# Placing the loaded rows of a convolution on other partitions, in more and partly longer transfers

## The chip, the cores and the metric

The kernel runs on one core of one Trainium2 chip. The metric is device time in microseconds (us) of one execution. Each kernel was run several times; the profile of one of those executions is read below. An execution that took over 1.5% longer than the fastest of its kernel is called slow, the others fast; comparisons are between fast ones. The granted clock is the share of full speed that TensorE's clock was granted, as the profile shows it.

Engines are named as in the profile: PE is TensorE's matmuls and PEld its weight loads, DVE is VectorE, ACT ScalarE, POOL GpSimd, SP SyncE. SPq, ACTq and so on are the sequencers that issue DMA transfers. A line number such as L174 is a line of the kernel profiled, so the same code has another number in another kernel.

## The reference, cut to what matters

```python
# x (8, 5696, 128), h (5696, 128), float32
Xf = np.fft.rfft(x, n=2 * S, axis=1)
Hf = np.fft.rfft(h, n=2 * S, axis=0)
y = np.fft.irfft(Xf * Hf[None], n=2 * S, axis=1)[:, :S, :]     # long convolution
x2 = y.reshape(8 * 5696, 128)
logits = x2 @ phi                                               # 32 slots
d = softmax over the 45568 rows;  slot_input = d.T @ x2
slot_out = relu(slot_input @ w1[e]) @ w2[e]                     # per expert
c = softmax over the slots;       out = c @ slot_out            # (45568, 128)
```

## The kernel before

The convolution is done as matrix products over 5,696 = 89 x 64 rows. One *step* handles one chunk of one sequence: it loads x (89 rows to 89 partitions, two runs of 2 KB each), folds it on GpSimd, multiplies it on TensorE and stores the result f to memory. A second stage loads f again as g, multiplies with the transform of h and stores z. A third stage loads z (90 rows) for two chunks at a time and goes on from there; two steps are a *pair*. There are 72 steps (h, then eight sequences of eight chunks) and 32 pairs of the third stage. Nearly all transfers are issued by SP.

```python
SPLIT = R1 // 16 * 16                    # 80 of R1 = 89 rows
Z0, X0, F0, F1 = 20, 20, 6, 82           # first partitions
...
xcs = [apool.tile([P, 2, CH, D], F32, name=f"xc{i}", ...) for i in range(3)]
def load_x(c):
    ...
    for r in (slice(0, SPLIT), slice(SPLIT, R1)):        # 80 rows, then 9
        v = src[r, CH * j:CH * (j + 1), :]
        v = bass.AP(tensor=v.tensor, offset=v.offset,
                    ap=[v.ap[0], [gap * D, 2], [1, CH * D]])
        nc.sync.dma_start(
            out=t_[X0 + r.start:X0 + r.stop, :, :, :].rearrange("p s n d -> p s (n d)"), in_=v)
...
def stage_b2(u):
    ...
    st = bpool.tile([P, 2, 2 * D], F32, name="zst", tag="zst", bufs=3)
    nc.scalar.activation(st[:, 0:n, :], bz[:, 0:n, 0:2 * D], AF.Copy)
    nc.sync.dma_start(out=zd[g - 1]..., in_=st[:, 0:n, :])          # the z store
...
def load_z(c):                                            # one chunk, 90 rows, runs of 8 KB
    ...
    nc.sync.dma_start(out=t_[Z0:Z0 + N1, :, :, :, :]..., in_=zd[b]...[:, j * w_:(j + 1) * w_])

def load_pair(T):
    if T < NT:
        load_z(2 * T)
        load_z(2 * T + 1)
...
for t in range(steps):
    ...
    if pair(1 - 2 * ahead) is not None:
        load_pair(pair(1 - 2 * ahead))                    # z, in every second step
    if t < NA:
        load_x(t + 3)                                     # x of three steps later
        stage_a(t, 0)                                     # its f stores come next
        fold(t + 1, 0)
    ...
```

The order of the calls is the order on SP's queue: first z, then x, then the f stores, then loads of g and stores of z. In the trace of before, its 977 transfers, 973 of SP and 4 of ScalarE, name eight completion semaphores strictly in turn, and 914 of SP's 973 wait, in the instruction or just ahead of it, for the semaphore that they then name, which is that of the transfer eight before. I read this as at most **eight in flight**.

Of the kernel before, what the change touches and what calls it, by code (L numbers as in the profile page):

```python
# [10 lines left out]
F32 = mybir.dt.float32  # L11
# [3 lines left out]
PSUM = bass.MemoryType.PSUM  # L15


def transform_tables(S, N1, N2, CH, Z0, X0, F0, F1):












    N, R1, HALF, P = N1 * N2, S // N2, N2 // 2, 2 * N2
    k1 = np.arange(N1)
    alpha = np.pi * (k1 + 0.5) / N1
    m1 = np.arange(R1) - (N1 - 1) / 2
    a1 = np.outer(m1, alpha)
    s1 = np.stack([np.cos(a1), -np.sin(a1), -np.cos(a1)], 1)
    a0 = np.outer(alpha, np.arange(N1 // 2) + 0.5)
    i1 = np.stack([np.cos(a0), -np.sin(a0), -np.cos(a0)], 1)
    NP = N1 // 2
    part = s1  # L40
    s1 = np.zeros((P, 3, P))
    for a, p in enumerate((F0, F1)):
        s1[X0:X0 + R1, :, p:p + NP] = part[:, :, a * NP:(a + 1) * NP]
    i1 = np.pad(i1[np.arange(N1).reshape(2, N1 // 2).T.reshape(-1)],
                [(Z0, P - N1 - Z0), (0, 0), (0, N2 - N1 // 2)])
    k2 = np.arange(N2)
    omega = np.pi * (k1[:, None] + 2 * N1 * k2[None] + 0.5) / N
    m2 = np.arange(HALF) - (N2 - 1) / 2
    a2 = m2[None, :, None] * omega[:, None, :]
    w = np.concatenate([np.cos(a2), np.sin(a2)], 1)  # L50
    back = np.arange(N2).reshape(2, HALF // CH, CH).transpose(1, 0, 2).reshape(-1)
    NU = (NP + 1) // 2
    turn = (N1 - 1) / 2 * alpha[:, None] + (N2 - 1) / 2 * omega
    wq = np.zeros((2, N2, NP, N2))
    vq = np.zeros((2, N2, NU, 2, N2))
    tn = np.zeros((2, N2, 2, NU, 2))
    for a in range(2):
        wq[a] = w[a * NP:(a + 1) * NP].transpose(1, 0, 2)
        for q in range(NP):
            vq[q % 2, :, q // 2, a] = w[a * NP + q][back].T  # L60
            tn[q % 2, :, 0, q // 2, a] = np.cos(turn[a * NP + q]) / N
            tn[q % 2, :, 1, q // 2, a] = np.sin(turn[a * NP + q]) / N
    wq, vq, tn = [t.reshape(P, *t.shape[2:]) for t in (wq, vq, tn)]
    return [np.ascontiguousarray(t, dtype=np.float32) for t in (s1, i1, wq, vq, tn)]
# [3 lines left out]
def kernel(  # L68
# [24 lines left out]
    nc = tc.nc  # L93
    P = 128
    B, S, D = x.shape
    NSL = moe_phi.shape[1]
    E, _, F = moe_w1.shape
    SPE = NSL // E
    NFC = F // P
    N1, N2 = 90, 64  # L100
    R1, HALF, NP = S // N2, N2 // 2, N1 // 2
    CH = 4
    NJ = HALF // CH
# [4 lines left out]
    HP = P // 2  # L108
    NQ = NJ // 2
    assert S == R1 * N2 and R1 == N1 - 1 and D == P and CH == Q == 4  # L110
    SPLIT = R1 // 16 * 16
    Z0, X0, F0, F1 = 20, 20, 6, 82
    ctx.enter_context(tc.manual_schedule())

    t_s1, t_i1, t_w, t_v, t_turn = [
        nc.inline_tensor(t, f"tab_{n}").ap()
        for n, t in zip(("s1", "i1", "w", "v", "turn"), transform_tables(S, N1, N2, CH, Z0, X0, F0, F1))]
    fd = [nc.dram_tensor(f"f_{g}", (2, N2, NP, 2, D), F32, kind="Internal").ap() for g in range(B + 1)]
    zd = [nc.dram_tensor(f"z_{b}", (NP, 2 * N2, 2, D), F32, kind="Internal").ap() for b in range(B)]
    cd = nc.dram_tensor("c_t", (P, B * NQ, Q, 2, MH), F32, kind="Internal").ap()  # L120
# [42 lines left out]
    def load_x(c):  # L163
        if c >= (B + 1) * NJ:
            return
        g, j = divmod(c, NJ)
        src = (h if g == 0 else x[g - 1]).rearrange("(a n) d -> a n d", n=N2)
        t_ = xcs[c % len(xcs)]
        gap = N2 - CH * (2 * j + 1)
        for r in (slice(0, SPLIT), slice(SPLIT, R1)):  # L170
            v = src[r, CH * j:CH * (j + 1), :]
            v = bass.AP(tensor=v.tensor, offset=v.offset,
                        ap=[v.ap[0], [gap * D, 2], [1, CH * D]])
            nc.sync.dma_start(  # L174
                out=t_[X0 + r.start:X0 + r.stop, :, :, :].rearrange("p s n d -> p s (n d)"), in_=v)
        xs[c] = t_

    folded = {}
# [100 lines left out]

    zs, ys, Ls, ds = {}, {}, {}, {}  # L280
    ybufs = [ypool.tile([P, Q * CH, D + 1], F32, name=f"y{i}") for i in range(2)]
    zring = [ypool.tile([P, 2, CH, 2, D], F32, name=f"zc{i}") for i in range(2)]
    lt = ypool.tile([P, CH, 2, HP], F32, name="lt")
    dt = ypool.tile([P, CH, 2, HP], F32, name="dt")
    om, op = [ypool.tile([P, CH, D], F32, name=n) for n in ("om", "op")]
    yt = ypool.tile([D, Q * CH, 2, MH], F32, name="yt")
    for t_ in zring:
        nc.vector.memset(t_[:, :, :, :, :], 0.0)
    for t_ in (lt, dt):
        nc.vector.memset(t_[:, :, :, :], 0.0)  # L290
    for t_ in ybufs:
        nc.vector.memset(t_[:, :, D:D + 1], 1.0)

    def load_z(c):
        b, j = divmod(c, NJ)
        t_ = zring.pop(0)
        zring.append(t_)
        w_ = 2 * CH * 2 * D
        nc.sync.dma_start(
            out=t_[Z0:Z0 + N1, :, :, :, :].rearrange("k o n c d -> k (o n c d)"),  # L300
            in_=zd[b].rearrange("q (a r) c d -> (q a) (r c d)",
                                a=2)[:, j * w_:(j + 1) * w_])
        zs[c] = t_

    def load_pair(T):
        if T < NT:
            load_z(2 * T)
            load_z(2 * T + 1)

    def stage_c1(T, between):  # L310
        za, zb = zs.pop(2 * T), zs.pop(2 * T + 1)
        y_ = ybufs[T % 2]

        def part(v, f):
            k = (2 * v + f) * CH
            return y_[:, k:k + CH, 0:D] if f == 0 else y_[:, k + CH - 1:k - 1:-1, 0:D]

        def product(o, tab, q):
            p = bank()
            for h_, t_ in enumerate((za, zb)):  # L320
                nc.tensor.matmul(p[h_ * HP:(h_ + 1) * HP, :], i1[:, tab, :], t_[:, o, :, q, :],  # L321
                                 start=True, stop=True)
            return p[:, :].rearrange("p (n d) -> p n d", d=D)

        def fold_out(even, minus, plus):
            nc.vector.tensor_tensor(out=plus, in0=even, in1=minus, op=AL.add)  # L326
            nc.vector.tensor_tensor(out=minus, in0=even, in1=minus, op=AL.subtract)

        b_, a_ = product(0, 1, 1), product(0, 0, 0)
        nc.scalar.activation(part(0, 0), b_, AF.Copy)  # L330
        fold_out(a_, part(0, 0), part(1, 0))
        between()
        b_, a_ = product(1, 1, 0), product(1, 2, 1)
        nc.scalar.activation(om[:, :, :], b_, AF.Copy)

        def after():
            fold_out(a_, om[:, :, :], op[:, :, :])
            for v, o_ in ((1, op), (0, om)):
                for part_, sign in ((part(v, 1), AL.subtract), (part(v, 0), AL.add)):
                    nc.gpsimd.tensor_tensor(out=part_, in0=part(v, 0), in1=o_[:, :, :], op=sign)  # L340

        ys[T] = y_
        return after
# [194 lines left out]
    for t in range(steps):  # L538
# [74 lines left out]
        if t == last_front:  # L613
# [4 lines left out]
            tail["cT"] = last.tile([P, B, R1, 2 * NJ], F32, name="cT")  # L618
            tail["pool"] = cload.enter_context(tc.tile_pool(name="cload", bufs=3))
            w2s = last.tile([P, E, NFC, D], F32, name="w2s")  # L620
            for i in range(2):
                t_ = last.tile([P, 2, CH, 2, D], F32, name=f"zd{i}")
                nc.vector.memset(t_[:, :, :, :, :], 0.0)
                zring.insert(i, t_)
            assert pair(1) is not None
            load_pair(pair(1) + 2)
            ahead = 2
# [147 lines left out]
```

## Time and profile before

| | before |
|---|---|
| time, median of 3 runs | 1003.1 us (999.5 to 1004.2) |
| profiled execution | 1011.1 us (span of the profile 1009.3), granted clock 0.934 |
| start of step 27 | 206.7 us |
| mean length of steps 27 to 71 | 11.79 us |
| transfers issued by SP | 973 in the whole kernel; from 250 to 700 us there are 505, and issuing them takes 0.57 of that time |

A step contains eight matmuls of the line `bank<-x,s`, so the start of every eighth of them gives the start of a step.

The second is the view of one tile's instructions: count, then shortest, median and longest duration in nanoseconds, then the first and last start in us. In these timelines a wait for a semaphore stands ahead of the issue that it holds up and not in its duration, so I read the median duration as the time that the sequencer itself needs; why single issues take over 1 us is not shown.

```profile
L174 SPq DMA_DIRECT2D xc<-in_x_dram x128: 294/388/1570, 31.8 to 697.1; - x128
L299 SPq DMA_DIRECT2D zc<-z x60: 327/454/1439, 189.7 to 857.1; - x60
```

From 250 to 700 us the median issue takes SP 0.33 to 0.46 us, depending on the tile. The timeline of SP in one step of the middle (start, duration of the group, what) shows a z load, an x load and two f stores issued in under 3 us:

```profile
470.82 0.78 SPq L299 DMA_DIRECT2D zc<-z  x2
471.65 1.10 SPq L174 DMA_DIRECT2D xc<-in_x_dram  x2
472.80 0.80 SPq L202 DMA_DIRECT2D f<-fst  x2
```

### The profile page before, as it was taken

What the parts mean: (1) busy time and instruction counts of PE and PEld (TensorE: products, weight loads), DVE (VectorE), ACT (ScalarE), POOL (GpSimd) and SP (SyncE); (2) the same over time, 40 slices, a digit from 0 to 9 for tenths busy, and PEclk for the clock granted to TensorE, in tenths of its full rate; (3) what the DMA queues carried; (4) which work ended last, traced back from release to release, by engine and by line L of the source; (5) the groups of instructions that cost most, each with busy time, mean ns of one, the idle gap of its engine ahead of it and who ended that gap; (6) DMA issues with size and microseconds to landing.
All of it is one profiled execution on the core that took longest, in us unless ns stands there. A gap on an engine that the chain in (4) does not pass through costs nothing.

```text
span 1009.3 us, 20225 instructions
## 1 busy us (share of the span) xinstructions
PE 868.0 (86%) x7220; PEld 426.4 (42%) x7220; DVE 662.0 (66%) x1137; ACT 520.0 (52%) x1051; POOL 462.2 (46%) x427
## 2 busy tenths in 40 slices
PE   6777788799999999999999999999978787675893
PEld 2222233234444444444444444444544433433783
DVE  2034577468877877877887777878867785353552
ACT  3557544355665556655555555665644443342442
POOL 5546533245555555555555545555532222784000
PEclk9989999899999999999999999999998898785955
DMA  6998899899989999999999899999988885951598
GB/s 187 268 266 268 262 327 305 254 304 295 289 280 299 287 275 305 294 291 268 310 306 285 265 301 294 277 294 298 291 236 256 241 245 155 259 181 62 195 404 330
DMA packets 177283, 272.79 MB, mean 270 GB/s; under 512 B 15024, under 2 KB 119728, under 8 KB 171423
## 3 DMA queue, kind: packets, MB, share of 16 engines
q1 hardware_dynamic: 176607, 271.13, 87.2%
q8 instruction: 58, 0.95, 0.4%
q10 hardware_dynamic: 576, 0.36, 0.2%
q14 instruction: 42, 0.34, 0.1%
HBM read 143.04 MB, written 128.39 MB: 269 GB/s over the span
## 4 chain that ended last, share of the span: by engine, by line
PE 43%; DMA 18%; POOL 16%; DVE 13%; issue 5%; ACT 2%; SPq 2%; DVEq 0%; ACTq 0%; POOLq 0%
POOL y L340 15%; PE bank L196 11%; PE bank L321 7%; PE bank L349 7%; PE bt L229 7%; DMA z<-zst 7%; DMA out_dram<-o 4%; PE bz L269 4%; DMA gt<-f 4%; DVE yf L255 2%; DVE pr L250 2%; DVE pi L253 2%; PE bank L359 2%; DMA zc<-z 2%; DVE op L326 2%
## 5 line engine op out<-in xcount | busy, mean ns | idle before, releaser
L196 PE MATMUL bank<-x,s 128*128 128x512 f32 x576 | 286.7, 625 | 10.0 <-DMA xc<-in_h_dram 8.4
L185 POOL TENSOR_TENSOR x<-xc 128x512 f32<-128x512 f32 x144 | 183.4, 1274 | 165.6 <-PE bank L196 132.5
L273 ACT ACTIVATE zst<-bz 128x512 f32<-128x512 f32 (+1 forms) x184 | 108.2, 588 | 206.2 <-PE bz L269 148.0
L198 ACT ACTIVATE fst<-bank 128x512 f32<-128x512 f32 x288 | 168.3, 597 | 87.2 <-PE bank L196 68.6
L250 DVE TENSOR_TENSOR pr<-bt,Hr 128x512 f32<-128x512 f32 (+1 forms) x184 | 126.4, 687 | 126.0 <-PE bt L229 122.5
L229 PE MATMUL bt<-gt,wt 64*64 64x256 f32 x1620 | 139.9, 409 | 41.0 <-DMA gt<-f 11.2
L196 PEld LDWEIGHTS bank<-x,s 128*128 128x128 f32 x576 | 100.4, 193 | 133.0 <-issue 88.6
L255 DVE TENSOR_TENSOR yf<-pr,pi 128x512 f32<-128x512 f32 (+1 forms) x184 | 150.6, 818 | 6.4
L321 PE MATMUL bank<-zc,i 128*64 128x512 f32 x480 | 122.5, 607 | 10.2 <-ACT y L330 7.3
L253 DVE TENSOR_TENSOR pi<-bt,Hi 128x512 f32<-128x512 f32 (+1 forms) x184 | 125.0, 679 | 0.0
L269 PE MATMUL bz<-yf,vt 64*64 64x256 f32 x1440 | 118.1, 383 | 6.8 <-DVE yf L255 4.1
L349 PE MATMUL bank<-ident,y 128*128 128x128 f32 x512 | 76.8, 314 | 42.4 <-POOL y L340 42.4
L229 PEld LDWEIGHTS bt<-gt,wt 64*64 64x64 f32 x1620 | 45.0, 134 | 158.8 <-PE bank L196 53.5
L340 POOL TENSOR_TENSOR y<-y,op 128x512 f32<-128x512 f32 x64 | 75.7, 1182 | 57.4 <-DVE op L326 54.9
L350 ACT ACTIVATE yt<-bank 128x360 f32<-128x360 f32 x128 | 57.9, 471 | 69.4 <-PE bank L349 69.4
L349 PEld LDWEIGHTS bank<-ident,y 128*128 128x128 f32 x512 | 68.1, 163 | 56.1 <-POOL y L340 56.1
L340 POOL TENSOR_TENSOR y<-y,om 128x512 f32<-128x512 f32 x64 | 85.2, 1332 | 2.5
L396 POOL MEMSET dt<- 64x8 f32 x32 | 3.4, 107 | 175.8 <-ACT dn L399 98.8
L269 PEld LDWEIGHTS bz<-yf,vt 64*64 64x64 f32 x1440 | 55.6, 134 | 42.2 <-issue 10.2
L240 DVE SCALAR_TENSOR_TENSOR Hr<-bt,turn,ph 128x128 f32<-128x128 f32 (+1 forms) x46 | 16.1, 349 | 76.5 <-ACT ph L238 76.5
L370 DVE TENSOR_REDUCE mx<-lt 64x1 f32<-64x360 f32 x64 | 32.9, 515 | 40.4 <-ACT lt L362 40.0
L321 PEld LDWEIGHTS bank<-zc,i 128*64 128x64 f32 x480 | 30.4, 135 | 67.3 <-issue 37.6
(95 smaller groups left out, 905.5 us busy)
## 6 DMA issues: line engine op xcount, KB each, us to landing
f<-fst SPq DMA_DIRECT2D x288, 180.0 KB
gt<-f SPq DMA_DIRECT2D x198, 256.0 KB
z<-zst SPq DMA_DIRECT2D x176, 256.0 KB
zc<-z SPq DMA_DIRECT2D x60, 720.0 KB
xc<-in_x_dram SPq DMA_DIRECT2D x64, 320.0 KB
out_dram<-o SPq DMA_DIRECT2D x16, 1024.0 KB
out_dram<-o SPq DMA_DIRECT2D x8, 768.0 KB
c_t<-cst SPq DMA_DIRECT2D x26, 180.0 KB
```

Of the source, the lines that this page charges most:

```text
L185: nc.gpsimd.tensor_tensor(out=y_[:, :, :], in0=t_[:, 0, :, :], in1=t_[:, 1, ::-1, :], op=AL.subtract if comp else AL.add)
L196: nc.tensor.matmul(p[:, :], s1[:, tab[G], :], src[:, :, :].rearrange("p n d -> p (n d)"), start=True, stop=True)
L198: nc.scalar.activation(st[:, :, G, :], p[:, :].rearrange("p (n d) -> p n d", d=D), AF.Copy)
L229: nc.tensor.matmul(bt[q * HP:(q + 1) * HP, a, 0:2 * D], wt[r, 2 * i + q, :], t_[r, q, :, :].rearrange("p c d -> p (c d)"), start=True, sto ...
L250: nc.vector.tensor_tensor(out=pr[r, :, :, :], in0=pv, in1=Hr[r, i, :, :].unsqueeze(2).broadcast_to([n * HP, 2, 2, D]), op=AL.mult)
L253: nc.vector.tensor_tensor(out=pi[r, :, :, :], in0=pv, in1=Hi[r, i, :, :, :], op=AL.mult)
L255: nc.vector.tensor_tensor(out=y_[r, :, :, :], in0=pr[r, :, :, :], in1=pi[r, :, ::-1, :], op=AL.add)
L269: nc.tensor.matmul(bz[a * HP:(a + 1) * HP, q, 0:2 * D], vt[r, i, a, :], y_[r, a, :, :].rearrange("p c d -> p (c d)"), start=True, stop=True)
L273: nc.scalar.activation(st[:, 0:n, :], bz[:, 0:n, 0:2 * D], AF.Copy)
L321: nc.tensor.matmul(p[h_ * HP:(h_ + 1) * HP, :], i1[:, tab, :], t_[:, o, :, q, :], start=True, stop=True)
L340: nc.gpsimd.tensor_tensor(out=part_, in0=part(v, 0), in1=o_[:, :, :], op=sign)
L349: nc.tensor.transpose(p[:, i * P:(i + 1) * P], ys[T][:, k * CH + i, 0:D], ident[:, :])
```

## The change

The intent is to shorten the packets of x and z by other places for their rows: 64 rows go to partitions 32 to 95, the others in groups of eight, four partitions apart. What the trace of before shows is that packets to the old places, rows from partition 20 on, are long for their size: z's of 8,192 bytes take 502 ns in the mean (400 to 700 us) and 309 at the 10th percentile, while the 2,048-byte packets of the output stage, whose transfers span 128 partitions, take 84. That the places are why is my assumption, the port step; no trace shows a cause. x then takes five transfers a step where it took two. The z of both chunks of a pair is read in one run of 16 KB per row, so z takes five transfers a pair where it took two. The tables that are multiplied with these rows are permuted to match.

```diff
+def row_blocks(n):                     # (first row, rows, first partition, partition step)
+    blocks = [(0, 64, 32, 1)]
+    for i, r in enumerate(range(64, n, 8)):
+        blocks.append((r, min(8, n - r), i, 4))
+    assert len(blocks) <= 5
+    return blocks
 ...
-        for r in (slice(0, SPLIT), slice(SPLIT, R1)):
-            v = src[r, CH * j:CH * (j + 1), :]
+        for r, n, p, step in row_blocks(R1):
+            v = src[r:r + n, CH * j:CH * (j + 1), :]
 ...
             nc.sync.dma_start(
-                out=t_[X0 + r.start:X0 + r.stop, :, :, :].rearrange("p s n d -> p s (n d)"), in_=v)
+                out=t_[p:p + step * (n - 1) + 1:step, :, :, :].rearrange("p s n d -> p s (n d)"),
+                in_=v)
 ...
-    zring = [ypool.tile([P, 2, CH, 2, D], F32, name=f"zc{i}") for i in range(2)]
+    zring = [ypool.tile([P, 2, 2, CH, 2, D], F32, name="zc")]
 ...
-    def load_z(c): ...                 # one transfer of 90 rows, 8 KB each; twice a pair
+    def load_pair(T):
+        ...
+        w_ = 2 * 2 * CH * 2 * D
+        for r, n, p, step in row_blocks(N1):
+            nc.sync.dma_start(
+                out=t_[p:p + step * (n - 1) + 1:step, :, :, :, :, :].rearrange(
+                    "k h o n c d -> k (h o n c d)"),
+                in_=zd[b].rearrange("q (a r) c d -> (q a) (r c d)",
+                                    a=2)[r:r + n, j * w_:(j + 1) * w_])
 ...   (tables s1 and i1 permuted; matmuls read t_[:, h_, o, :, q, :])
```

More of the change, by code (lines that the diff above doesn't have):

```diff
@@ L15, with partitions, transform_tables @@
 PSUM = bass.MemoryType.PSUM
-def transform_tables(S, N1, N2, CH, Z0, X0, F0, F1):
+def row_blocks(n):
[4 more added lines that the diff above has]
+    return blocks
+def partitions(n):
+    return np.concatenate([p + step * np.arange(k) for _, k, p, step in row_blocks(n)])
+def transform_tables(S, N1, N2, CH, F0, F1):
     N, R1, HALF, P = N1 * N2, S // N2, N2 // 2, 2 * N2
@@ L42, in transform_tables @@
     for a, p in enumerate((F0, F1)):
-        s1[X0:X0 + R1, :, p:p + NP] = part[:, :, a * NP:(a + 1) * NP]
-    i1 = np.pad(i1[np.arange(N1).reshape(2, N1 // 2).T.reshape(-1)],
-                [(Z0, P - N1 - Z0), (0, 0), (0, N2 - N1 // 2)])
+        s1[partitions(R1), :, p:p + NP] = part[:, :, a * NP:(a + 1) * NP]
+    part = i1
+    i1 = np.zeros((P, 3, N2))
+    i1[partitions(N1), :, 0:NP] = part[np.arange(N1).reshape(2, NP).T.reshape(-1)]
     k2 = np.arange(N2)
@@ L110 @@
     assert S == R1 * N2 and R1 == N1 - 1 and D == P and CH == Q == 4
-    SPLIT = R1 // 16 * 16
-    Z0, X0, F0, F1 = 20, 20, 6, 82
+    F0, F1 = 6, 82
     ctx.enter_context(tc.manual_schedule())
@@ L116 @@
         nc.inline_tensor(t, f"tab_{n}").ap()
-        for n, t in zip(("s1", "i1", "w", "v", "turn"), transform_tables(S, N1, N2, CH, Z0, X0, F0, F1))]
+        for n, t in zip(("s1", "i1", "w", "v", "turn"), transform_tables(S, N1, N2, CH, F0, F1))]
     fd = [nc.dram_tensor(f"f_{g}", (2, N2, NP, 2, D), F32, kind="Internal").ap() for g in range(B + 1)]
@@ L286 @@
     yt = ypool.tile([D, Q * CH, 2, MH], F32, name="yt")
-    for t_ in zring:
-        nc.vector.memset(t_[:, :, :, :, :], 0.0)
+    nc.vector.memset(zring[0][:, :, :, :, :, :], 0.0)
     for t_ in (lt, dt):
@@ L292 @@
         nc.vector.memset(t_[:, :, D:D + 1], 1.0)
-    def load_z(c):
-        b, j = divmod(c, NJ)
+    def load_pair(T):
+        if T >= NT:
+            return
+        b, j = divmod(T, NQ)
         t_ = zring.pop(0)
         zring.append(t_)
-        w_ = 2 * CH * 2 * D
-        nc.sync.dma_start(
-            out=t_[Z0:Z0 + N1, :, :, :, :].rearrange("k o n c d -> k (o n c d)"),
-            in_=zd[b].rearrange("q (a r) c d -> (q a) (r c d)",
-                                a=2)[:, j * w_:(j + 1) * w_])
-        zs[c] = t_
-    def load_pair(T):
-        if T < NT:
-            load_z(2 * T)
-            load_z(2 * T + 1)
+        w_ = 2 * 2 * CH * 2 * D
[5 more added lines that the diff above has]
+                                    a=2)[r:r + n, j * w_:(j + 1) * w_])
+        zs[T] = t_
     def stage_c1(T, between):
-        za, zb = zs.pop(2 * T), zs.pop(2 * T + 1)
+        t_ = zs.pop(T)
         y_ = ybufs[T % 2]
@@ L319, in product @@
             p = bank()
-            for h_, t_ in enumerate((za, zb)):
-                nc.tensor.matmul(p[h_ * HP:(h_ + 1) * HP, :], i1[:, tab, :], t_[:, o, :, q, :],
-                                 start=True, stop=True)
+            for h_ in range(2):
+                nc.tensor.matmul(p[h_ * HP:(h_ + 1) * HP, :], i1[:, tab, :],
+                                 t_[:, h_, o, :, q, :], start=True, stop=True)
             return p[:, :].rearrange("p (n d) -> p n d", d=D)
@@ L620 @@
             w2s = last.tile([P, E, NFC, D], F32, name="w2s")
-            for i in range(2):
-                t_ = last.tile([P, 2, CH, 2, D], F32, name=f"zd{i}")
-                nc.vector.memset(t_[:, :, :, :, :], 0.0)
-                zring.insert(i, t_)
+            t_ = last.tile([P, 2, 2, CH, 2, D], F32, name="zd")
+            nc.vector.memset(t_[:, :, :, :, :, :], 0.0)
+            zring.insert(0, t_)
             assert pair(1) is not None
```

## The prediction

> **What bounds the kernel now.** I read the page first (busy digits and DMA row), then busy time by stretches, the waits of the middle, the chain, and the DMA-issuing queue.
>
> ```profile
> PE 868.0 (86%) x7220; PEld 426.4 (42%) x7220; DVE 662.0 (66%) x1137; ACT 520.0 (52%) x1051; POOL 462.2 (46%) x427
> ...
> PE   6777788799999999999999999999978787675893
> ...
> DMA  6998899899989999999999899999988885951598
> ...
> q1 hardware_dynamic: 176607, 271.13, 87.2%
> ```
>
> The digits show two resources at nine tenths from slice 9 to slice 29: TensorE and the sixteen DMA engines. The table by stretches (us, then busy time of PE, PEld, DVE, ACT, POOL, clock, DMA share, GB/s) gives sizes:
>
> ```profile
> 100.00:150.00 50.00, 40.72 (x272) 15.71 (x276) 30.40 (x58) 26.96 (x59) 20.93 (x20) 0.97 0.94 293
> 150.00:190.00 40.00, 31.38 (x229) 11.98 (x220) 25.44 (x39) 17.18 (x30) 11.02 (x9) 0.95 0.92 288
> ...
> 250.00:400.00 150.00, 143.90 (x1223) 67.67 (x1221) 119.27 (x196) 89.14 (x172) 82.14 (x73) 1.00 0.95 290
> 400.00:550.00 150.00, 145.58 (x1236) 68.52 (x1236) 118.71 (x194) 90.51 (x174) 81.93 (x71) 1.00 0.97 292
> ...
> 840.00:930.00 90.00, 57.88 (x413) 35.62 (x413) 39.81 (x79) 32.04 (x80) 55.42 (x63) 0.77 0.57 175
> ```
>
> From 250 to 550 us PE works 289.5 of 300 us at full clock while DMA is busy 0.96. Only the first of these can set the pace directly; the waits (waiter, releaser, total us, times, longest) of the middle, 250 to 700 us, say how much of PE's time is lost, and the whole span's list where DMA reaches compute:
>
> ```profile
> PE bank L349 <- POOL y L340: 11.5, 19, 1.0
> PE bank L321 <- ACT y L330: 6.0, 7, 1.8
> ```
>
> ```profile
> ACT zst L273 <- DMA z<-zst: 49.7, 17, 4.5
> ```
>
> PE lost 17.5 of 450 us, and no DMA is named; but ScalarE waits 17 times for a z store to land before it may reuse a staging buffer. The chain that ended last (start, us, what) carries the same stores, and two loads of z that compute waits for:
>
> ```profile
> 190.12 8.84 DMA zc<-z
> ...
> 308.89 10.51 DMA z<-zst
> ...
> 842.25 9.67 DMA zc<-z
> ```
>
> Taking the start of every eighth matmul of L196 from the instruction records gives the step: most steps between 198 and 725 us are 11.47 to 11.63 us, with odd ones at 12.0 to 13.6. So the middle is **paced by TensorE with a nearly saturated DMA system behind it**, and DMA surfaces as late stores and loads. The output stage (945 us on) is DMA alone and the change does not touch it.
>
> **Why DMA is so busy.** I grouped the trace's packet records by size. In the output stage, all of it transfers over 128 partitions, a 2,048-byte packet takes 84 ns (mean 85). In 400 to 700 us the 2,048-byte packets are 107 ns in the mean: g loads, over 128 partitions, are about two thirds of them, so at 84 ns for those the x packets come to about 155 ns, which is also the 90th percentile (156). The z loads' 8,192-byte packets take 502 ns in the mean, 309 at the 10th percentile. At 840 to 930 us, with DMA only 0.57 busy, they still take 519. Their slowness is therefore their own, not a queue's.
>
> [...]84 and 159 ns (4,096 bytes, median) for 128-row loads against 155 and 502 for the shifted ones; ports are in no record.
>
> **The change part by part.** The unit is a pair of steps, 23.4 us in the middle.
>
> [...]the mean is 22.3, or 0.95, which is the measured share.[...]
>
> After, [...](84 ns; for 16,384 bytes I take 609 ns, an estimate from 159 and 309 ns for 4,096 and 8,192): [...]mean 18.3, a DMA share near 0.79. [...]the mean gains 4.
>
> Added: x goes from two issues a chunk to five (72 chunks: +216), z from two a pair to five (32 pairs: +96). One issue on the queue took 0.3 us at best:
>
> ```profile
> 405.58 0.33 SPq L470 DMA_DIRECT2D c_t<-cst  x1
> ...
> 413.07 0.87 SPq L174 DMA_DIRECT2D xc<-in_x_dram  x2
> ...
> 422.08 0.91 SPq L299 DMA_DIRECT2D zc<-z  x2
> ```
>
> 312 x 0.35 us = 109 us more work for the issuing queue, which I add up at 57% of its time in the middle: 9 x 0.36 = 3.3 us a pair more makes 71%. It hides there. At the start, where x and f steps last about 3.5 to 4.4 us, nine issues at 0.36 take 3.2 us, so nothing is gained and the first x chunk comes 3 issues, 1 us, later. Engine instructions, tiles and memory stay the same.
>
> What lies on the path: middle steps, excess over 11.55 us summed from the list of steps, about 10 us net of catch-ups; I count 7 as recoverable, and 3 more if the regular step shortens by 0.07. Two steps at 173 to 198 us take 12.8 against 8.3 just before, 9 us together, made of late z stores and the first z load. [...]I give 2 us there, 2 for the stores. The z wait at 842 us likewise 2. Stage borders 1. Start -1 to -2. Sum about **15 us**: 1003 - 15 = 988.
>
> **Rivals.** *TensorE is already the floor*: PE is 96% busy in the middle, so all DMA relief is hidden; only the two z-load waits gain, 4 us, time 999. For it: PE names no DMA wait. Against it: chain and the 12 to 13.6 us steps. *The issue queue or its eight completion semaphores become the wait*: the program gives each transfer one of eight semaphores in turn and makes it wait for the transfer eight before. Five small pieces of x now take five of the eight slots for 356 KB, and five of z then five of x stop everything behind them until z lands. 35.75 transfers a pair leave 5.2 us per transfer for eight slots, against 7.0 before. For it: z stores took 8 to 10.5 us to land in the chain. Against it: that was backlog, which shrinks. If it wins, 1005 to 1025. *DMA was the real pacemaker*: [...]every pair could approach 22.6 us, the shortest seen. 22 pairs x 0.8 = 18 us and the rest as above: 970 to 978. Against it: 11.16 us steps occur only after a stall.
>
> **Range and chances.** My sum sits between the first and third rivals; the second is the only way to lose. 8 in 10: 973 to 1001. Faster by over 2% (under 983) needs most of the third: 0.28. Within 2%: 0.67. Slower: 0.05.
>
> **What would show each step.** DMA share in 250 to 700 us near 0.8, x packets near 85 ns and 16,384-byte packets near 610 prove the port step; packets staying at 155 ns or twice 500 refute it. The wait of ScalarE for z stores should fall well below 49.7 us; the z waits at 190 and 842 should drop by about 2 us. PE should be at 97 to 98% in the middle. The issue queue should spend most of its growth on x lines. Wrong would be: [...]transfers waiting for semaphores so that DMA idles; or a step that falls well below 11.5 us, meaning DMA held TensorE up in gaps too short to be listed.

## More of the kernel before

The prediction shows the main lines of this profile. Two more matter for what follows. The first is a line of the page: the shares that each engine, sequencer or DMA has in the chain of work that ended last.

```profile
PE 43%; DMA 18%; POOL 16%; DVE 13%; issue 5%; ACT 2%; SPq 2%; DVEq 0%; ACTq 0%; POOLq 0%
```

SP's sequencer is 2% of the chain: in this execution issuing transfers hardly ever decides when something happens.

## The result, and the profile after

| | before | after |
|---|---|---|
| time, median of 4 runs | 1003.7 us (999.5 to 1004.7) | 1105.8 us (1101.4 to 1107.2) |
| ratio after / before, 95% interval | | 1.102 (1.097 to 1.106) |
| start of step 27 | 206.7 us | 245.8 us |
| mean length of steps 27 to 71 | 11.79 us | 13.18 us |
| SP: transfers in the whole kernel | 973 | 1285 |
| SP: transfers and issuing share, 250 to 700 us | 505, 0.57 | 604, 0.84 |
| granted clock, profiled execution | 0.934 | 0.909 |

A ratio in this document is the mean time of one kernel's fast runs over that of the other's fast runs of the same rounds, so it is not quite the ratio of the medians beside it.

The change cost 10%. The table of steps says where: 39 us before step 27 begins, and 44 steps x 1.39 us = 61 us from there to step 71. Together that is 100 us, where the two profiled executions differ by 96, so the end of the kernel has not become slower.

The same lines of the page as the prediction shows of before, with the chain's shares added:

```profile
PE 899.7 (81%) x7220; PEld 434.5 (39%) x7220; DVE 661.5 (60%) x1135; ACT 515.7 (47%) x1051; POOL 460.6 (42%) x427
...
PE   5757777787899899989889897999797787566894
...
DMA  5677787888888887888788888887898775644299
...
q1 hardware_dynamic: 175326, 271.14, 76.6%
...
PE 42%; DMA 29%; SPq 9%; POOL 8%; DVE 5%; issue 4%; ACT 3%; ACTq 0%; DVEq 0%; POOLq 0%
```

TensorE no longer stands at nine tenths through the middle, and the DMA engines nowhere in it: both now wait for something else. In the chain, SP's sequencer went from 2% to 9% and DMA from 18% to 29%. The table by stretches has, after the stretch and its length, busy time of PE, PEld, DVE, ACT and POOL, then clock, DMA share and GB/s:

```profile
100.00:150.00 50.00, 38.02 (x195) 13.13 (x193) 22.44 (x63) 29.18 (x77) 26.20 (x26) 0.90 0.78 233
250.00:400.00 150.00, 132.04 (x1050) 60.46 (x1052) 100.50 (x166) 75.78 (x148) 69.26 (x60) 0.96 0.82 261
400.00:550.00 150.00, 137.34 (x1100) 62.60 (x1100) 106.32 (x174) 80.30 (x157) 74.45 (x65) 0.96 0.82 259
```

The DMA share fell from 0.95 and 0.97 to 0.82, as the prediction wanted, but the bytes per second fell with it, from about 291 to 260 GB/s. Share times length gives the mean busy time of a DMA engine in a pair of steps: 22.6 us before and 21.8 after, where 18.3 was predicted. The engines are hardly relieved; they are fed more slowly. The waits of the compute engines agree (waiter, releaser, total us, times, longest):

```profile
ACT zst L288 <- DMA z<-zst: 153.3, 44, 7.8
...
PE bt L244 <- DMA gt<-f: 43.9, 19, 11.7
...
POOL x L200 <- DMA xc<-in_x_dram: 39.0, 9, 10.2
```

ScalarE's wait for z stores, which was to fall well below 49.7 us, tripled. The loads of g and x come late as well. Three kinds of transfer are late at once, and two of them the change doesn't touch, so I looked at what they share, SP's queue. Tile by tile, with the durations in nanoseconds as before:

```profile
L188 SPq DMA_DIRECT2D xc<-in_x_dram x320: 413/677/1784, 42.4 to 798.9; - x160
L316 SPq DMA_DIRECT2D zc<-z x150: 538/603/1777, 227.9 to 960.8; - x150
```

A piece of x takes 677 ns to issue at the median, where a piece before, larger, took 388. The timeline of one z step:

```profile
463.06 3.22 SPq L316 DMA_DIRECT2D zc<-z  x5
466.38 5.37 SPq L188 DMA_DIRECT2D xc<-in_x_dram  x5
471.85 0.89 SPq L217 DMA_DIRECT2D f<-fst  x2
473.17 0.35 SPq L230 DMA_DIRECT2D gt<-f  x1
```

Where before took 2.8 us for z, x and f together, this takes 9.7. Five issues of x at 0.67 us are 3.3 us, so some 2 us of the x group's 5.37 is waiting inside it. It sits ahead of the fourth piece of x (issued at 470.40 us, 1.85 us after the third had ended), which is the transfer eight after the first piece of z and names the same semaphore. SP's own waits name it (whole span of after), and the chain has loads of z in it again and again:

```profile
SPq L188 <- DMA zc<-z: 28.8, 20, 2.5
```

```profile
231.32 6.32 DMA zc<-z
...
465.07 6.80 DMA zc<-z
```

**Summed up for a pair of the middle.** From 250 to 700 us after, a pair lasts 26.4 us, of which SP spends 0.84 or 22.2 us issuing; before it spent 13.3 of 23.6 us. The difference is 8.9 us. The mean issues of that stretch give its parts: x from 2 x (0.47 + 0.50) = 1.9 to 2 x 3.31 = 6.6 us (five pieces of 0.65, 0.72, 0.67, 0.67 and 0.59), z from 0.9 to 3.3 us, and the transfers that the change left alone 1.7 us, since their issues got longer too (a g load 0.61 to 0.77, an f store 0.42 to 0.50). The rest of the 26.4 is gaps of 50 to 110 ns between issues, waits for loads of z like the one above, 0.67 us a step in the mean, and 0.2 us of other waits.

Such waits for z are not new, though. Before, they stood ahead of other transfers, above all of loads of g (L215) and stores of z (L274):

```profile
SPq L215 <- DMA zc<-z: 38.6, 16, 3.4
SPq L274 <- DMA zc<-z: 37.4, 14, 3.7
```

In sum SP waited 105.3 us for loads of z before and 35.7 us after (2.2 and 0.67 us a step in the middle). What is gone is its slack: outside its issues, SP's waits for anything else than z fell from 2.0 to 0.2 us a step. In the changed kernel SP is full, of issues and not of waits.

**Why an issue got slower.** The trace gives the issue time by shape (medians over the whole kernel). Before: 386 ns for 80 rows of x in two runs, 403 for nine, 454 for 90 rows of z. After: for x in two runs 663 for 64 rows, 677 for eight rows in steps of four, 621 for a single row; for z 588 for 64 rows, 603 for eight, 567 for its last two. Nine pieces of x, a single row in one run each, took 408 to 417; none of the other 511 pieces of x and z took under 538. At the start of the kernel, where little else is in flight, most issues of an x load took 0.31 to 0.37 us before and 0.62 to 0.73 after. The unchanged loads of h without what I call the *mark*, which a switch of the build, `nc.dge_precook = False`, takes away (e1), took 0.60 us at least and 0.77 at the median, and five pieces in the old places (e13) 0.31 and 0.42. So the new pieces issue like transfers without the mark, and I call them unmarked, and transfers that issue in about 0.4 us marked; the traces show the times alone, and why these shapes take longer is not shown.

### The profile page after: what moved, and what is told of

It is laid out like the page before. It is cut to its first block, busy times and chain, and to the rows that moved or that the text cites. A ratio compares the mean times of both kernels' runs of the same rounds, so it can differ in the third digit from the quotient of the medians.

```text
span 1105.1 us, 20703 instructions
## 1 busy us (share of the span) xinstructions
PE 899.7 (81%) x7220; PEld 434.5 (39%) x7220; DVE 661.5 (60%) x1135; ACT 515.7 (47%) x1051; POOL 460.6 (42%) x427
## 4 chain that ended last, share of the span: by engine, by line
PE 42%; DMA 29%; SPq 9%; POOL 8%; DVE 5%; issue 4%; ACT 3%; ACTq 0%; DVEq 0%; POOLq 0%
PE bank L211 12%; DMA zc<-z 8%; DMA z<-zst 8%; PE bt L244 7%; PE bank L334 7%; DMA gt<-f 6%; POOL y L353 6%; PE bz L284 4%; PE bank L362 4%; DMA out_dram<-o 3%; SPq L188 3%; SPq L217 2%; SPq L316 2%; DMA f<-fst 2%; PE bank L372 1%
## 5 line engine op out<-in xcount | busy, mean ns | idle before, releaser
L211 PE MATMUL bank<-x,s 128*128 128x512 f32 x576 | 303.8, 657 | 18.9 <-ACT fst L213 10.6
L200 POOL TENSOR_TENSOR x<-xc 128x512 f32<-128x512 f32 x144 | 188.9, 1312 | 214.8 <-PE bank L211 130.9
L244 PE MATMUL bt<-gt,wt 64*64 64x256 f32 x1620 | 145.7, 424 | 59.3 <-DMA gt<-f 43.9
L211 PEld LDWEIGHTS bank<-x,s 128*128 128x128 f32 x576 | 106.8, 205 | 152.7 <-issue 102.6
L334 PE MATMUL bank<-zc,i 128*64 128x512 f32 x480 | 125.0, 631 | 44.2 <-ACT y L343 31.2
L270 DVE TENSOR_TENSOR yf<-pr,pi 128x512 f32<-128x512 f32 (+1 forms) x184 | 146.9, 798 | 6.4
L284 PE MATMUL bz<-yf,vt 64*64 64x256 f32 x1440 | 124.6, 401 | 8.6 <-DVE yf L270 3.9
L339 DVE TENSOR_TENSOR y<-bank,y 128x512 f32<-128x512 f32 x32 | 22.0, 688 | 61.5 <-ACT y L343 58.8
```

The costliest lines, as they stand in the source:

```text
L200: nc.gpsimd.tensor_tensor(out=y_[:, :, :], in0=t_[:, 0, :, :], in1=t_[:, 1, ::-1, :], op=AL.subtract if comp else AL.add)
L211: nc.tensor.matmul(p[:, :], s1[:, tab[G], :], src[:, :, :].rearrange("p n d -> p (n d)"), start=True, stop=True)
L244: nc.tensor.matmul(bt[q * HP:(q + 1) * HP, a, 0:2 * D], wt[r, 2 * i + q, :], t_[r, q, :, :].rearrange("p c d -> p (c d)"), start=True, sto ...
L270: nc.vector.tensor_tensor(out=y_[r, :, :, :], in0=pr[r, :, :, :], in1=pi[r, :, ::-1, :], op=AL.add)
L284: nc.tensor.matmul(bz[a * HP:(a + 1) * HP, q, 0:2 * D], vt[r, i, a, :], y_[r, a, :, :].rearrange("p c d -> p (c d)"), start=True, stop=True)
L334: nc.tensor.matmul(p[h_ * HP:(h_ + 1) * HP, :], i1[:, tab, :], t_[:, h_, o, :, q, :], start=True, stop=True)
```

## The experiments

Two theories came out of this. **Issue time**: SP has to spend more time, because there are more issues, and the new ones issue like transfers without the mark. **Eight in flight**: the pieces take up the eight places, so a queue in strict order stands behind a z load until it lands. A third, **contention** (in the expectations: uneven engines, or the new rows), was that the new places are themselves worse for the DMA engines. Most kernels give x and z a list of pieces each, (first row, rows, first partition, step); only the lists are shown then. Time is the median of the fast runs, the ratio is to the kernel before of the same rounds.

### e1: the kernel before, all marks off

```diff
     nc = _bacc.Bacc("TRN2", target_bir_lowering=False, num_devices=1)
+    nc.dge_precook = False
```

> The kernel before with every transfer built without the mark[...] (the build has a switch for it); nothing else differs. In the two profiles an unloaded x issue took 0.31 us with the mark and 0.62 us without. Issue-time theory (the issuing queue has become the pacemaker): 26.75 issues a pair at 0.28 us more each fill the queue to about 0.89 of its time, as much as in the changed kernel (0.84), so 1060 to 1110 us, with one issue never under 0.5 us. Too-many-pieces theory (eight completion semaphores) and uneven-engines theory: the pieces and rows are those of before, so 1000 to 1015 us.

1099.5 us, 1.092 (1.085 to 1.099). The tile view of x:

```profile
L174 SPq DMA_DIRECT2D xc<-in_x_dram x128: 592/796/1633, 37.9 to 787.6; - x128
```

The same transfers to the same places, issued in 796 instead of 388 ns, cost 9%. SP's issuing share from 250 to 700 us rises from 0.57 to 0.75 and the step from 11.79 to 13.26 us. So taking the mark away, without one more transfer, can cost what the change cost. That it acts through issue time alone is not quite shown: the traces do not tell when single transfers land, so a later landing of unmarked transfers is not excluded. Nor is it shown yet that it is what cost in the change.

### e2 and e3: x alone, z alone

```diff
 # e2                                              # e3
+x: row_blocks(89)                                 +x: [(0, 80, 20, 1), (80, 9, 100, 1)]
+z: as before, two transfers of 90 rows            +z: row_blocks(90), one tile a pair
```

> Only x moves to the new rows in five pieces; z is loaded as before. Issue-time theory: 10 issues of 0.66 us against 4 of 0.49 us a pair, 4.7 us more for a queue that has 10 us to spare, about half of the loss or more: 1035 to 1075 us. Pieces theory: most of the added pieces are x's (216 of 312): 1060 to 1090. Uneven-engines theory: [...]less than half: 1020 to 1045.

> Only z moves to the new rows and the one tile for both chunks, in five pieces; x is loaded as before. Issue-time theory: 5 issues of 0.66 us against 2 of 0.46 us a pair, 2.4 us more: 1005 to 1030 us. Pieces theory: 96 of 312 added pieces: 1020 to 1040. Uneven-engines theory: z carries most of the unevenness[...]: 1050 to 1090. If the port step of the prediction were all that counted: 990.

e2 took 1126.8 us, 1.117 (1.107 to 1.126); e3 took 987.1 us, 0.980 (0.974 to 0.986). The whole loss is x's, and z's half of the change is a gain of 17 us. e2 lies above every range that was written down for it; of those for e3 only the 990 fits, which supposes that the shorter packets are all that counts. The table by stretches, the wait of ScalarE for z stores, and the chain's shares in e3:

```profile
250.00:400.00 150.00, 146.24 (x1242) 68.87 (x1232) 118.56 (x195) 90.53 (x173) 83.75 (x73) 1.00 0.93 294
```

```profile
ACT zst L293 <- DMA z<-zst: 29.5, 18, 3.3
```

```profile
PE 52%; POOL 17%; DMA 11%; DVE 10%; issue 4%; ACT 2%; SPq 1%; DVEq 0%; ACTq 0%; POOLq 0%
```

PE is busy 97.5% of that stretch, the wait fell from 49.7 to 29.5 us, DMA's share of the chain from 18 to 11%, and the steps from 27 on from 11.79 to 11.51 us: the picture that the prediction painted for the whole change, but for the DMA share, which is 0.93 and not 0.79. Sorted by size, the 16,384-byte packets of z take 754 ns in the mean and 620 at the median (400 to 700 us).

### e4 and e5: x in more pieces in the old places, and the same with x ahead of z

e4 leaves the rows where they were and cuts the 80 into five transfers of 16. e5 issues x ahead of z as well, so that z's load is younger when its place is wanted.

```diff
+x: [(16 * i, 16, 20 + 16 * i, 1) for i in range(5)] + [(80, 9, 100, 1)]      # e4 and e5
 # e5 also:
+        if t < NA:
+            load_x(t + 3)
         if pair(1 - 2 * ahead) is not None:
             load_pair(pair(1 - 2 * ahead))
         if t < NA:
-            load_x(t + 3)
             stage_a(t, 0)
```

> The kernel before, its x rows at their old partitions, but loaded in six contiguous pieces (five of 16 rows, one of 9) that all keep the mark. More pieces (288 more transfers than before, against 312 in the change)[...]. Issue-time theory: 8 issues a pair at 0.36 to 0.45 us more, 3 to 3.6 us: 1005 to 1030 us. Pieces theory: as slow as the change or nearly, 1060 to 1110. Uneven-engines theory: 1000 to 1010.

> The six-piece kernel of e4 with one thing moved: in a step that loads z, the x pieces are issued ahead of the z load instead of behind it; same transfers, same bytes. Eight-in-flight theory: in e4 z and six x pieces filled all eight places, and the f stores behind them waited for z to land (124 us, 47 times); now six other transfers can be issued while z is under way, so that wait should shrink to under 40 us and the time fall from 1130 to 1030 to 1080 us. Issue-time theory: the same issues in another order, 1115 to 1135.

e4 took 1129.7 us, 1.121 (1.114 to 1.128), e5 1079.0 us, 1.071 (1.063 to 1.078). SP's waits of e4, then of e5:

```profile
SPq L221 <- DMA zc<-z: 124.3, 47, 3.8
```

```profile
SPq L221 <- DMA zc<-z: 66.9, 36, 3.8
```

In e4 the six pieces of x at 442 us of the trace are issued in 2.97 us, 0.50 each, the places are the old ones, and SP issues for only 0.67 of the time; still it loses 12%, more than either theory expected. Dear issues can't explain that, nor can new places, and a full queue of issues isn't needed for it: e7 and e14 below issue for 0.66 and 0.83 of the time and lose 0 and 2%. What it shows is the f store standing behind z's load for 124 us. The reordering of e5 nearly halves that wait and takes five points, about 50 us, off the time, less than was expected of it (a wait under 40 us). Waiting for z in a queue of eight places is a cost of its own.

### e6: the whole change, x ahead of z

The same move of one line in the changed kernel.

> The changed kernel with the same move: x pieces ahead of z pieces. Eight-in-flight theory: places freed by small x pieces come back sooner than z's, 1050 to 1085 us. Issue-time theory: the queue is 0.84 full of issues either way, so 1095 to 1115.

1132.4 us, 1.124 (1.118 to 1.130): slower than the change, where the eight-in-flight theory had it faster. SP's waits tell why:

```profile
SPq L193 <- POOL x L205: 59.4, 28, 4.0
```

x now comes first and must wait until GpSimd has folded the chunk whose buffer it takes; z's five pieces (in after about 0.6 us each to issue) wait behind that. The order of a queue trades one wait for another, so the number that the theory gave for this run was wrong (the issue-time theory's 1095 to 1115 was missed too), and the run does not decide between the theories.

### e7 and e8: the new places with few transfers, z's long runs in the old places

```diff
 # e7: 64 rows, and the last 32 again (of which the first few are not used)
+x: [(0, 64, 32, 1), (57, 32, 0, 1)]         +z: [(0, 64, 32, 1), (58, 32, 96, 1)]
 # e8
+x: as before                                +z: [(0, 90, 20, 1)], one tile a pair
```

> The change with two pieces each for x and z instead of five: 64 rows in the middle as in the change, and the last 32 rows in one contiguous piece (x at partitions 0 to 31, z likewise), so that some rows arrive twice and the second copy meets zeros in the tables. Issues: 0.65 + 0.35 us. Both queue theories: about as many transfers as before and little more issue time, so the loss goes: 975 to 1000 us. If the new rows themselves were what costs[...]: still over 1030.

> The kernel before with only the last part of the change: both chunks of z in one transfer of 90 rows at the old partitions, 16 KB runs, x as before. If the 2% that e3 gained come[...]: no gain here, 995 to 1008 us, and 16 KB packets near 1000 ns. If they come from one transfer fewer and longer runs: 980 to 992.

e7 took 1011.5 us, 1.003 (0.998 to 1.009), and e8 1014.3 us, 1.008 (1.001 to 1.016). With two pieces for each load the loss of 102 us shrinks to nothing that can be told from zero, though the 64-row pieces (0.66 us to issue in after) are still there; the gain down to 975 to 1000 us that was expected did not come. e8, a little above the 995 to 1008 expected if the new rows are what e3 gains by, separates the two halves of z's change: in the old places the 16,384-byte packets take 1033 ns in the mean, 1088 at the median, against 754 and 620 in e3 (400 to 700 us). So length alone gains nothing; the new rows do, placement and cut together. In e7, where 64 of z's rows lie as in the change and 32 contiguously, the packets take 941 and 821 ns.

### e9, e10 and e14: the change with x issued from another engine

```diff
-            nc.sync.dma_start(
+            nc.gpsimd.dma_start(          # e9, and e14, which also has SP's marks all off
+            nc.scalar.dma_start(          # e10
```

> The changed kernel, every row and piece as it is, but the five x pieces of a chunk are issued from GpSimd's queue[...]: the Sync queue is relieved both of 10 issues of 0.66 us a pair and of the places among its eight. Queue theories (issue time or eight in flight): the loss goes as far as GpSimd's own issuing lets it, 985 to 1040 us. If x's new rows themselves cost[...]: 1080 or more, as e2 against before.

> The changed kernel with the x pieces issued from ScalarE's queue, which draws on the same eight semaphores. The Sync queue loses 6.6 us of issue time a pair, the eight in flight stay. Issue-time theory: 1000 to 1060 us, ScalarE having 11 us a pair to spare. Eight-in-flight theory: 1090 or more, with ScalarE now held up at x issues that wait for z to land.

> e9 (x issued from GpSimd's queue) with every transfer of the Sync queue built without the mark. The eight places are as free as in e9 (1015 us). Issue-time theory: 19 issues a pair at 0.28 to 0.38 us more fill the queue again, 1060 to 1110 us. Eight-in-flight theory: 1010 to 1030.

e9 took 1015.4 us, 1.007 (1.000 to 1.013). GpSimd's transfers stand on a queue of their own in the trace (q0, 14,976 packets), and none of SP's seven longest waits is for a transfer of x. Its tile view and its middle stretch:

```profile
L193 POOL DMA_DIRECT2D xc<-in_x_dram x320: 503/567/721, 42.3 to 702.7; - x160
```

```profile
400.00:550.00 150.00, 146.99 (x1240) 68.54 (x1236) 127.27 (x201) 91.77 (x175) 117.56 (x137) 1.00 0.94 303
```

The same pieces to the same partitions, off SP's queue, give steps of 11.49 us and 303 GB/s. So **the new places are not worse**, and with e4, which loses as much in the old ones, contention falls as a cause. (GpSimd's queue also forms its packets otherwise: an x row's two runs stand in the trace as one packet of 4,096 bytes.) What e9 still loses lies before step 27, which begins at 228.6 us, with steps of 5.70 us in h's part. Five issues at 0.57 us and two folds at 1.3 us would fill 5.5 us of GpSimd there, which fits, but no run tests it.

e10 took 1306.4 us, 1.295 (1.287 to 1.304). ScalarE's transfers take turns on the eight semaphores with SP's, as its four do in the trace of before, and ScalarE also computes. So SP stops for x's transfers of the other queue, 128.8 us ahead of f stores and 92.0 ahead of z stores, and ScalarE's copies stop for them too, 302.7 us: the eight-in-flight theory's side (1090 or more), and far from the issue-time theory's 1000 to 1060. The worst wait says so:

```profile
ACT fst L218 <- DMA xc<-in_x_dram: 302.7, 59, 10.3
```

e14 took 1023.9 us, 1.017 (1.010 to 1.024). Its middle stays near e9's, 11.64 us a step, although every issue that is left to SP is dear and SP issues for 0.83 of the time, as in after:

```profile
400.00:550.00 150.00, 146.09 (x1236) 68.02 (x1233) 123.53 (x197) 90.52 (x173) 120.48 (x141) 1.00 0.93 298
```

With x's pieces out of SP's order, dear issues cost the middle 0.15 us a step; in e1, with x in it, they cost 1.47. SP's waits for z give way instead (1.5 us a step in e9, 0.6 in e14). The two limits are not independent: it is one queue, and what either takes is missing for the other.

### e11, e12, e13, e15, e16 and e17: z as in e3, and x varied

The best kernel so far, e3, is the clean base for asking what x's pieces cost. Each of these has z in the new places.

```diff
 # e11: x as before, its marks off
 # e12: x in one transfer of 90 rows where a next row exists (7 of 8 sequences)
+x: [(0, 90, 20, 1)]
 # e13: five contiguous pieces
+x: [(0, 32, 20, 1), (32, 16, 52, 1), (48, 16, 68, 1), (64, 16, 84, 1), (80, 9, 100, 1)]
 # e15: three contiguous pieces
+x: [(0, 48, 20, 1), (48, 32, 68, 1), (80, 9, 100, 1)]
 # e16: x as before, marks of x and of the f stores off
 # e17: e3 again, five rounds
```

> The z part of the change alone (as e3), with the two old x pieces a chunk built without the mark: 4 issues a pair at about 0.25 us more, 1 us. In e3 the queue issued for 0.71 of the time and waited for compute besides, so issue-time theory gives no or a small loss: 985 to 1000 us. If an unmarked transfer were harmful in itself (later landing, other engines): 1010 or more.

> A version meant to win: z as in the change, x in one marked transfer of 90 rows (the 90th row belongs to the next batch and meets zeros in the table; h and the last batch keep two pieces). One issue and one place fewer a chunk. If the queue still costs something in e3: 975 to 985 us. If e3 stands at the compute floor, as its steps of 11.5 us suggest: 984 to 990.

> The changed kernel's z, and x in five pieces as in the change, but contiguous at the old partitions[...] (32, 16, 16, 16, 9)[...]. Issue-time theory: 10 issues at 0.40 instead of 0.66 us, 2.6 us a pair less than the changed kernel's 26 us, back at or near the compute pace of 23.1: 985 to 1015 us. Eight-in-flight theory: the places are as crowded as in the change: 1070 to 1120.

> z as in the change, x in three marked contiguous pieces (48, 32, 9 rows), one more a chunk than in e3 (987 us). Issue-time theory: 0.8 us more a pair in a queue with slack: 985 to 1000. Eight-in-flight theory: a step in the same direction, 1010 to 1040.

> e3 (z as in the change, x in its two old pieces) with the marks taken from x and from the f stores that follow it: 4 issues a pair at 0.28 us and 8 at 0.42 us more, 4.5 us of issue time a pair where e13 added 2.5, and no transfer more. Issue-time theory: at least e13's loss, 1080 to 1125 us. Eight-in-flight theory: much less than e13's, 1005 to 1045.

> e3 again in five rounds, to see whether the z part alone beats the kernel before by 2%: 983 to 991 us, ratio 0.975 to 0.986.

| run | x | time, us | ratio to before | step 27 starts, us | steps 27 to 71, us |
|---|---|---|---|---|---|
| e12 | one transfer | 989.2 | 0.979 (0.971 to 0.987) | 200.8 | 11.54 |
| e3 | two, marked | 987.1 | 0.980 (0.974 to 0.986) | 201.3 | 11.51 |
| e17 | two, marked, again | 989.0 | 0.979 (0.975 to 0.983) | 202.6 | 11.61 |
| e11 | two, unmarked | 1005.4 | 0.996 (0.990 to 1.002) | 210.1 | 11.72 |
| e15 | three | 1015.3 | 1.007 (1.000 to 1.014) | not given | not given |
| e16 | two, unmarked, f too | 1045.5 | 1.035 (1.031 to 1.040) | 227.7 | 12.12 |
| e13 | five, marked | 1080.7 | 1.072 (1.067 to 1.077) | 222.1 | 13.04 |
| after | five, unmarked | 1105.8 | 1.102 (1.097 to 1.106) | 245.8 | 13.18 |

One piece more (e15) costs about 28 us, three more (e13) 94 us, and the change's own five, unmarked and in the new places, another 25. The two old pieces without their marks (e11) cost 18 us. At 1005 us this lies between the two ranges written down for it, up to 1000 if the queue has slack and from 1010 if a missing mark does harm by itself, so it doesn't decide that. SP's waits and one step of its timeline in e13:

```profile
SPq L193 <- DMA zc<-z: 59.5, 33, 3.7
```

```profile
466.47 4.99 SPq L193 DMA_DIRECT2D xc<-in_x_dram  x5
```

Five issues whose median in this run is 418 ns take 5 us here, much like the 5.37 us of the change: time saved in issuing is spent waiting for z, in the same place. Hence the two stages part. Up to step 27, of the 44 us that after loses to e3, cheap issues (e13) give back 24, about half. From step 27 on, they give back 0.14 of the 1.67 us a step.

e16 checks whether it is only the sum of issue time that counts. It adds some 4.5 us a pair of issuing without a transfer more and loses 58 us to e3; e13 adds some 2.5 us a pair (six pieces at about 0.42) and loses 94. So pieces cost beyond their issue time.

What the slow runs have in common shows when SP's issues and its waits for z are added, per step from 250 to 700 us (summed from the traces afterwards; no run was planned on it):

| run | SP issues, us | waits for z, us | sum | other waits, us | step, us |
|---|---|---|---|---|---|
| before | 6.7 | 2.2 | 8.9 | 2.0 | 11.79 |
| e3 | 8.1 | 1.6 | 9.7 | 0.8 | 11.51 |
| e14 | 9.6 | 0.6 | 10.2 | 0.6 | 11.64 |
| e16 | 10.2 | 0.7 | 10.9 | 0.2 | 12.12 |
| e13 | 9.7 | 1.9 | 11.6 | 0.2 | 13.04 |
| after | 11.1 | 0.7 | 11.8 | 0.2 | 13.18 |
| e4 | 9.3 | 2.8 | 12.1 | 0.6 | 13.92 |

Neither column alone orders the steps; the sum does, once the other waits have shrunk to 0.2 to 0.6 us and SP has no slack left. In e16 longer issues cover waits for z; in e13, with three pieces more, those waits stay although SP issues longer. (e5 and e6, with x ahead of z, fit only with their waits for GpSimd, some 1.0 and 1.4 us, added; e10, with x on ScalarE's queue, doesn't fit.)

e12 asks whether still fewer transfers would help, and they don't: with PE at 97.5%, e3 stands where compute lets the middle go, as far as these runs show. e17 confirms e3 against eleven runs of the kernel before, at 1009.2 us. **The best version is z's half alone**, 987 to 989 us. That it is faster is clear; whether by more than 2% is not, since the interval of e17 ends at 0.983.

## Why the prediction was wrong, point by point

- **The cost of issuing was mis-sized.** The step that failed reads "312 x 0.35 us = 109 us more work for the issuing queue, which I add up at 57% of its time in the middle: 9 x 0.36 = 3.3 us a pair more makes 71%. It hides there." The count was right, and so was 57%; "It hides there" is what failed, since SP's slack of 2.0 us a step was used up. The price was taken from the shortest issue of the kernel before, a transfer of another shape. The pieces took 0.59 to 0.78 us each, the old transfers beside them got slower as well, and a pair got 8.9 us more, which makes 84%. e1 shows that missing marks alone can reach a loss of this size, and e13 that of the 119 us between after and e3 only about 25 come back with cheap issues (in old places), because SP then waits for z: 1.9 us a step where it was 0.7.
- **The second rival was put aside for a bad reason.** "Against it: that was backlog, which shrinks." Its first half, the issue queue, is what after shows; its second, the eight semaphores, is what cheap issues run into. The prediction counted the slots (5.2 us a transfer against 7.0), and the wait it described, "five of z then five of x stop everything behind them until z lands", is what the timeline of after shows at the fourth piece of x. A mean of 5.2 us hides that places are given in order: a z load of 6 to 7 us (6.32 and 6.80 in the chain of after) holds up the transfer eight after it, and SP waited 28.8 us in 20 waits for such loads at pieces of x alone. e4 shows 12% from more pieces (0.50 us each to issue) in the old places. The size given for it, 1005 to 1025, was too small as well, even without dear issues: e4 took 1130.
- **The start was mis-sized.** "Nothing is gained and the first x chunk comes 3 issues, 1 us, later" became 39 us to step 27. Steps of h's part went from 3.79 to 5.40 us. The nine issues of such a step, five of x and four of f, were put at 0.36 us each, 3.2 us. From 10 to 40 us after, their means are 0.58 to 0.72 us for x and 0.48 for f, together 5.2 us, which nearly fills the step. In e13 the same sum is 4.3 us, and the step 4.42.
- **The step about packets (the port step) was right for z's typical packet, but the DMA relief was mis-sized.** Predicted for a 16,384-byte packet were 609 ns; the median was 611 in after and 620 in e3, and 1088 in the old places (e8). But the mean, which a sum needs, was 715 and 754. With 754, z's 90 packets of a pair take 4.2 us of each of the sixteen engines in the mean, where 609 gives 3.4 and the 180 old ones of 502 gave 5.6, so of the 2.2 us that z was to gain 1.4 are left (estimates from these packet times). The mean engine was to fall from 22.3 to 18.3 us a pair, 1.6 of it by x's 356 packets at 84 instead of 155 ns; it measured 22.6 before, 21.8 in after, 21.4 in e3, and 21.1 in e9, where both loads lie in the new places and the middle runs at 11.49 us. The share of 0.82 in after came from idleness, not from relief: in e3 it was 0.93. That e3 gains 17 us where 15 were predicted for the whole change is in part luck.
- **For x the step is not shown, and its size was overestimated.** The 2,048-byte packets of 400 to 700 us, in which g loads are mixed, stayed at 84 ns in the median and went from 107 to 109 in the mean. The prediction took 84 ns for g loads and so came to 155 for x. In e9, where x has a queue of its own, the packets left on the other queue are g loads alone, and take 101 ns in the mean (84 at the median); with that, the same sum gives about 120 for x (an estimate). There x's packets of 4,096 bytes take 159 ns at the median, 187 in the mean, but e9 is no faster in the middle (11.49 us a step) than e3 with the old places (11.51).
- **The third rival did not come true.** In e3 the step stops at 11.5 us and PE at 97.5%; a further transfer less (e12) brings nothing. What any single DMA engine gained is in no record.

What stays open: why the 64-row and the stepped pieces take longer to issue, and what the mark changes besides the issue time; whether a transfer without the mark also lands later; what z's own five pieces cost within e3's gain; and how the 119 us divide between the two limits, since they share a queue and don't add up independently. The runs fix only the two ends: missing marks alone cost 9% (e1), cheap pieces alone 94 us (e13 against e3).

## What to carry to other kernels

Before cutting a transfer into pieces, add up the issuing queue as if it were an engine: number of pieces times the issue time *of that shape*, measured on a small program, and check how many transfers the program lets be in flight and what stands behind the slowest of them. The queue's issues and its waits for landings belong in one sum. When DMA share and GB/s fall together and waits for unrelated transfers grow, look at the sequencer that issues them, not at the DMA engines. And try each half of a change by itself: here one half was worth 2% and the other cost 12%.
